# Sliding-window attention and a gated feed-forward: a tail tile loaded and scored later, q and k transfers earlier in SP's queue

## The chip, the cores and the metric

One Trainium2 chip; the program runs on one of its cores. The metric is the device time of one execution in microseconds. Three runs of the kernel before gave 332.56 us as median (332.44 to 333.28). A difference of less than 0.3%, about 1.0 us, can't be told from no change.

The core has a matrix engine (TensorE, "PE"; its weight loads are listed as "PEld"), a vector engine (VectorE, "DVE"), an activation engine (ScalarE, "ACT"), GpSimd ("POOL") and SyncE ("SP"). POOL and SP are used here to issue transfers alone. Each issues in the order of its own queue, and an issue that has to wait holds all that stand behind it.

## The reference

```python
q, k, v: (8, 8, 576, 64)                       # batch, heads, positions, head size
scores = scale * q @ k^T                       # per batch and head
rel  = pos[:, None] - pos[None, :]
mask = (rel >= 0) & (rel < 128)                # causal, a window of 128
scores = where(mask, scores + slope[h] * -|rel|, -1e9)
attn = softmax(scores) @ v
x = attn as (8 * 576, 512)
g = x @ w_gate;  val = x @ w_val               # 512 -> 1536
out = (silu(g) * val) @ w_out                  # 1536 -> 512
```

## The kernel before, in words

**Tiles and units.** A batch has 576 positions: four tiles of 128 and a rest of 64. Batches are taken in pairs, `s` = 0 to 3. A pair has nine tiles of 128 rows: four of the one batch (p = 0 to 3), four of the other (p = 4 to 7), and one, p = 8, that holds the two rests, 64 rows of each: the **tail tile**. So there are 36 tiles; tile 9s + p has that number as its **rank**, and attention goes through them as **units** of the same numbers. Ranks 8, 17, 26 and 35 are tail tiles; 17 is that of batches 2 and 3.

**What a unit scores.** Keys of tile p are needed by the queries of tile p and of tile p + 1. A unit's pass multiplies its keys with two query tiles in one go (line 327, output `ps`), so unit 13 needs k 13, q 13 and q 14. Units with p = 3 and p = 7 end a batch and take one query tile (`scores_128`, line 394, output `psc`). The tail's queries are also scored against the last full tile of each batch (`scores_two`, line 359), and the tail against itself (`scores_128` once more, key `(s, "c")`). In pair 0 both stand at unit 8. In pairs 1 to 3 the tail against itself is scored along with unit p = 3, and `scores_two` along with unit p = 7; unit p = 8 then scores nothing, and its steps are empty lists. The scores go through ACT (exponential) and DVE (mask); `weighted` multiplies them with v, `x_transposed` puts the result into `xT`.

**Feed-forward.** It runs in blocks n = 0 to 8 of 512 rows: block 2s + b is one batch's four tiles, so block 3 takes units 13 to 16, and block 8 takes the four tail tiles. Each block multiplies `xT` with the gate and value weights (line 488), and its output projection (line 636) runs among the next block's products. Blocks 6 to 8 use other products (line 726). Attention and feed-forward are both generators, and `everything` deals out their steps: from step 60 on, attention gets 54 of its steps for 34.5 of the other's. From there PE's order is the order in which the program is written. What a unit yields, empty steps too, counts in this rate.

**How q, k and v come in.** POOL issues the loads (lines 191 and 197), rank by rank, at unit i up to rank i + 7 (`loads_to`); k and q go to staging tiles `kn` and `qn`, five of each. For a tail tile, `load_v` alone is called in its turn, and its k and q are loaded with rank 9s + 3 (`load_qk(rank + 5)`); those of rank 8 are written out by hand. A tail tile takes two transfers of 64 KB for each of k, q and v, another tile one of 128 KB.

From rank 11 on, k and q are transposed by transfers that SP issues (line 253), out of `kn` and `qn` into `kT` (12 places) and `qT` (9). `order` is the list of these transposes: in pair 0 the tail's stand at the end, in the others behind the first four tiles. `ahead(i)`, called at unit i, issues all that `due` puts at i + 4 or less (`AHEAD`); a tail's are due five ranks before their number, together with p = 3. `need[i]` says how many of the list must be out before unit i is scored.

**SP's queue** is written out by hand from unit 7 on: at each unit the transposes of `ahead(i)`, then the transposed result of unit i (line 451; units 8, 9 and from 13 on go this way, 10 to 12 through PE), then finished output rows (line 543).

Of the kernel before, what the change touches and what calls it, by code (L numbers as in the profile page):

```python
# [21 lines left out]
AHEAD = 4  # L22
# [13 lines left out]
SECOND = 5.5  # L36
RATE = 54.0
FIXED_FROM = 60
LATE = 13
VAL_COPIED_FROM = 2  # L40
CLOSE_TO = 13
# [15 lines left out]
def kernel(  # L57
# [65 lines left out]
    msk = consts.tile([P, H, P], FP16, name="m_c")  # L123
# [64 lines left out]
    def load_v(rank):  # L188
        va[rank] = va_all[rank % NV]
        for (p0, p1), src in source(v, rank):  # L190
            nc.gpsimd.dma_start(va[rank][p0:p1, :, 0:D], src)  # L191
# [40 lines left out]
    order = []  # L232
    for s in range(NSUP):
        tails = [("k", 9 * s + 8), ("q", 9 * s + 8)]
        for half in (0, 4):
            order += [(name, 9 * s + half + r) for name, r in zip("kqqkqkqk", (0, 0, 1, 1, 2, 2, 3, 3))]
            order += tails if half == (0 if s else 4) else []
    need = [18 * s + n for s in range(NSUP)
            for n in ((3, 5, 7, 10, 13, 15, 17, 18, 18) if s else (3, 5, 7, 8, 11, 13, 15, 16, 18))]

    def due(rank):

        return rank - 5 if rank % 9 == 8 and rank > 8 else rank

    last_qk = []

# [13 lines left out]
    def begin_scores(i, q4, par, pool=None, tag="a", bufs=4):  # L260

        ps = (pool or ps_a).tile([P, 2, 256], FP32, name="ps", tag=tag, bufs=bufs)
        begun[i, q4, par] = ps
        o = 4 * q4 + 2 * par
        nc.tensor.matmul(ps, idm, bias[:, o:o + 2, :], start=True, stop=False)
# [23 lines left out]
    def scores(i):  # L289

        s, p = units[i]
        def tails():
            return scores_128(s, 8, 8, (s, "c"), msk, unit=i, more=True)

        def together(one, two):
            return [one[0] + two[0]] + one[1:] + two[1:]

        if p == 8:
            return [[]] * 3 + (together(scores_two(s, i), tails()) if s == 0 else [[]] * 2)
        if p in (3, 7):  # L300
            own = scores_128(s, p, p, (s, p), reg[:, :, 0:P], i < FIRST, i)
            return own if s == 0 else together(own, tails() if p == 3 else scores_two(s, i, True))
        ks = (9 * s + p) % NK
        banks = []
        early_tile = i < FIRST
        e = epool.tile([P, H, 256], FP16, name="ex", tag="ex", bufs=4)
        ex[(s, p)] = e

        def products():
            scored[0] = True  # L310
            close.open()
            for q4 in range(2):
                if early_tile:
                    for n in ((q4, 1 - q4) if i < 2 else (q4,)):
                        for par in range(2):
                            if (i, n, par) not in begun:
                                begin_scores(i, n, par)
                    two = [begun[i, q4, par] for par in range(2)]
                else:
                    two = [ps_a.tile([P, 2, 256], FP32, name="ps", tag="a") for _ in range(2)]  # L320
                banks.append(two)
                for j in range(2):
                    pair = 2 * q4 + j
                    for par in range(2):
                        rows = slice(64 * par, 64 * par + 64)
                        with close.behind_first(i):
                            close.put(nc.tensor.matmul(two[par][:, j, :], kT[rows, ks, pair, :],  # L327
                                                       qT[rows, p:p + 2, pair, :],
                                                       start=(j == 0 and not early_tile), stop=(j == 1)))

        def act(q4, par):
            o = 4 * q4 + 2 * par
            nc.scalar.activation(e[:, o:o + 2, :], banks[q4][par], AF.Exp, scale=scale)  # L333

        def mul(q4):
            if early_tile:
                return
            o = slice(4 * q4, 4 * q4 + 4)
            nc.vector.tensor_mul(e[:, o, :], e[:, o, :], reg[:, o, :])  # L339

        return [[products], [lambda: act(0, 0)], [lambda: act(0, 1), lambda: mul(0)],
                [lambda: act(1, 0)], [lambda: act(1, 1), lambda: mul(1)]]

    def scores_two(s, i, more=False):

        ks = [(9 * s + kt) % NK for kt in (3, 7)]
        banks = []

        def products():
            scored[0] = True  # L350
            banks.extend(ps_a.tile([P, 4, P], FP32, name="psc", tag="a") for _ in range(2))
            if not more:
                close.open()
            for j in range(4):
                for n in range(2):
                    for par in range(2):
                        rows, half = slice(64 * par, 64 * par + 64), slice(64 * n, 64 * n + 64)
                        with close.behind_first(i):
                            close.put(nc.tensor.matmul(banks[par][:, j, half], kT[rows, ks[n], j, :],
                                                       qT[rows, 8, j, half], start=(j == 0 and n == 0),  # L360
                                                       stop=(j == 3 and n == 1)))

        def act(par):
            nc.scalar.activation(two_halves[:, 4 * par:4 * par + 4],
                                 banks[par].rearrange("k h (a q) -> k h a q", a=2), AF.Exp, scale=scale)

        def mul():
            nc.vector.tensor_mul(two_halves, two_halves, two_msk.unsqueeze(2).broadcast_to([P, H, 2, 64]))

        return [[products], [lambda: act(0)], [lambda: act(1), mul]]  # L370

    def scores_128(s, kt, qt, key, m, early_tile=False, unit=0, more=False):

        ks = (9 * s + kt) % NK
        banks = []
        e = epool.tile([P, H, P], FP16, name="exc", tag="exc", bufs=4)
        ex[key] = e

        er4 = e.rearrange("k (a par b) q -> k a par b q", a=2, par=2)

        def products():
            scored[0] = True
            banks.extend(ps_a.tile([P, 4, P], FP32, name="psc", tag="a") for _ in range(2))
            if not more:
                close.open()
            for par in range(2 if early_tile else 0):
                nc.tensor.matmul(banks[par].rearrange("k (a b) q -> k a b q", a=2), idm,
                                 bias.rearrange("k (a par b) q -> k a par b q", a=2, par=2)
                                 [:, :, par, :, 0:P], start=True, stop=False)
            for j in range(4):  # L390
                for par in range(2):
                    rows = slice(64 * par, 64 * par + 64)
                    with close.behind_first(unit):
                        close.put(nc.tensor.matmul(banks[par][:, j, :], kT[rows, ks, j, :], qT[rows, qt, j, :],
                                                   start=(j == 0 and not early_tile), stop=(j == 3)))

        def act(par):
            nc.scalar.activation(er4[:, :, par], banks[par].rearrange("k (a b) q -> k a b q", a=2),
                                 AF.Exp, scale=scale)

        return [[products], [lambda: act(0)],
                [lambda: act(1), lambda: early_tile or nc.vector.tensor_mul(e, e, m)]]
# [492 lines left out]
    loaded = done_t = 0  # L895

    def loads_to(r):
        nonlocal loaded
        while loaded <= min(r, NR - 1):
            rank = loaded  # L900
            if rank % 9 == 8:
                load_v(rank)
            else:
                load(rank)
            if rank % 9 == 3:
                load_qk(rank + 5)
            loaded += 1

    by_dma = [n for n in range(len(order)) if order[n][1] >= QK_DMA_FROM]
# [9 lines left out]

    def ahead(i):  # L920

        while by_dma and due(order[by_dma[0]][1]) <= min(i + AHEAD, loaded - 1):
            transpose(by_dma.pop(0))

    def run(steps):
# [46 lines left out]
    def attention():  # L972
# [5 lines left out]
        for i in range(FIRST, last + 1):  # L978
            late = i >= LATE
            if i == QUEUE_FROM:  # L980
# [77 lines left out]
    loaded = 11  # L1058
# [28 lines left out]
    def everything():  # L1087
# [13 lines left out]
        for step in steps:  # L1101
            if step >= FIXED_FROM and fixed is not None:
                fixed.enter_context(tc.manual_schedule(engines=ENGINES["pe"]))
# [50 lines left out]
```

## Time and profile before

| | |
|---|---|
| median of three runs | 332.56 us |
| the profiled execution | 333.68 us |
| its span, first to last instruction | 331.9 us |
| mean granted clock of TensorE | 0.997 |
| PE busy | 321.0 us, 2911 matmuls |
| DVE busy | 261.6 us |
| ACT busy | 221.4 us |
| loads by POOL's queue | 18.62 MB in 118880 packets |
| transfers by SP's and ACT's queues | 19.35 MB in 48048 packets |

The page cuts the span into 40 slices of 8.3 us and gives each engine's busy share in tenths. Its waits name for each engine the line that waited, what it waited for, the sum, the number of waits and the longest. A timeline line gives the start in us, the duration, the engine, the line of the kernel and the operation, output <- input, and in brackets the idle time ahead of it with what ended it; "xN" says that N instructions were merged into one line. SPq is SP's queue: its durations are those of issuing, and a transfer lands later. Landing times of single transfers come from the completion counts in the trace.

### The profile page before, as it was taken

The numbers are of one execution on the slowest core, as the hardware profiler recorded it, in microseconds if no ns is written. First come the engines' busy times: TensorE is split into PE (matmuls) and PEld (weight loads), VectorE is DVE, ScalarE is ACT, GpSimd is POOL, SyncE is SP. The second block draws the span as 40 slices with busy tenths as digits, with TensorE's granted clock in tenths as the row PEclk, the third lists the DMA queues.
The fourth block names the chain that finished last, engine by engine and source line by source line (L and its number), as shares of the span: only waits on it lengthen the run. The fifth ranks groups of instructions, "written<-read, shape, count | busy, mean of one in ns | idle before, by whom it ended". The sixth has DMA issues, their size and how long they took to land. (4 is left out here: it accounts for less than half of the span.)

```text
span 331.9 us, 7661 instructions
## 1 busy us (share of the span) xinstructions
PE 321.0 (97%) x2911; PEld 215.3 (65%) x2911; DVE 261.6 (79%) x638; ACT 221.4 (67%) x438; POOL 111.3 (34%) x138
## 2 busy tenths in 40 slices
PE   8999999999799999999999999999999999999994
PEld 4665465444356665656655655565788888888883
DVE  4678879999597689887998799997854976765783
ACT  4976777365586678777677768753577766777650
POOL 8967777396572535545335100000000000000000
PEclk9999999999999999999999999999999999999998
DMA  9999999999999999999999993113100101001014
GB/s 152 170 181 176 173 178 169 123 121 171 154 150 197 142 163 155 189 136 175 157 144 187 139 182 81 46 28 85 65 32 34 64 2 63 34 35 64 2 63 129
DMA packets 167654, 39.09 MB, mean 118 GB/s; under 512 B 155456, under 2 KB 163264, under 8 KB 167616
## 3 DMA queue, kind: packets, MB, share of 16 engines
q0 software_dynamic: 118880, 18.62, 79.2%
q1 hardware_dynamic: 48048, 19.35, 33.9%
q10 hardware_dynamic: 688, 0.62, 0.6%
q8 instruction: 23, 0.38, 0.5%
q14 instruction: 15, 0.12, 0.1%
HBM read 37.91 MB, written 9.44 MB: 143 GB/s over the span
## 5 line engine op out<-in xcount | busy, mean ns | idle before, releaser
L488 PE MATMUL pv<-xT,wv_sb 128*128 128x512 f16 (+2 forms) x312 | 76.6, 363 | 0.3 <-DVE uu L507 0.2
L488 PE MATMUL pg<-xT,wg_sb 128*128 128x512 f16 (+2 forms) x324 | 76.5, 355 | 0.4 <-DVE hT L515 0.3
L506 ACT ACTIVATE tt<-pg 128x512 f16<-128x512 f32 x68 | 41.7, 614 | 26.5 <-PE pg L488 25.1
L333 ACT ACTIVATE ex<-ps 128x512 f16<-128x512 f32 x96 | 51.0, 612 | 7.6 <-PE ps L327 7.6
L507 DVE SCALAR_TENSOR_TENSOR uu<-tt,pg 128x512 f16<-128x512 f16 x67 | 45.7, 683 | 8.3 <-ACT tt L506 7.9
L197 POOL DMA_DIRECT2D kn<-in_k_dram x39 | 33.3, 854 | 44.0 <-DMA kT<-kn 31.9
L488 PEld LDWEIGHTS <-wg_sb 128*128 128x128 f16 x324 | 29.6, 98 | 26.2 <-issue 2.6
L636 PEld LDWEIGHTS <-hT 128*128 128x128 f16 x384 | 37.0, 98 | 10.0 <-issue 1.0
L488 PEld LDWEIGHTS <-wv_sb 128*128 128x128 f16 x312 | 27.4, 98 | 22.9 <-issue 2.3
L520 ACT CAST hT<-pv 128x512 f16<-128x512 f32 x44 | 26.0, 592 | 19.4 <-PE pv L488 19.3
L197 POOL DMA_DIRECT2D qn<-in_q_dram x39 | 33.3, 860 | 15.4 <-DMA qn<-in_q_dram 8.5
L191 POOL DMA_DIRECT2D va<-in_v_dram x40 | 34.2, 861 | 10.6 <-DMA va<-in_v_dram 4.1
L339 DVE TENSOR_TENSOR ex<-ex,m_reg 128x1024 f16<-128x1024 f16 x42 | 28.9, 689 | 7.7 <-ACT ex L333 7.5
L636 PEld LDWEIGHTS <-S 128*128 128x128 f16 x288 | 27.6, 98 | 7.9 <-issue 1.1
L432 DVE TENSOR_TENSOR x<-av,rec 128x256 f16<-128x256 f32 x72 | 29.0, 421 | 0.6
L636 PE MATMUL po<-T,hT 128*128 128x256 f16 x192 | 26.1, 273 | 0.0
L636 PE MATMUL po<-T,S 128*128 128x256 f16 x192 | 25.9, 273 | 0.0
L521 DVE TENSOR_TENSOR hT<-uu,hT 128x512 f16<-128x512 f16 x44 | 18.5, 421 | 4.0 <-ACT hT L520 3.8
L780 DVE TENSOR_TENSOR hT<-s,v 128x512 f16<-128x512 f16 x18 | 7.6, 424 | 17.7 <-ACT s L779 17.7
L428 PEld LDWEIGHTS <-ex 128*128 128x128 f16 x384 | 17.6, 98 | 5.7 <-issue 1.2
L428 PE MATMUL av<-va,ex 128*128 128x65 f16 x384 | 19.2, 193 | 0.7 <-ACT ex L333 0.3
L327 PE MATMUL ps<-qT,kT 64*128 64x256 f16 x192 | 15.3, 271 | 2.8 <-DMA qT<-qn 2.0
(138 smaller groups left out, 556.4 us busy)
## 6 DMA issues: line engine op xcount, KB each, us to landing
out_dram<-osb SPq DMA_DIRECT2D x32, 256.0 KB, 2.3
va<-in_v_dram POOLq DMA_DIRECT2D x32, 128.0 KB, 10.3
qn<-in_q_dram POOLq DMA_DIRECT2D x31, 128.0 KB, 9.7
kn<-in_k_dram POOLq DMA_DIRECT2D x31, 128.0 KB, 8.6
wg_sb<-in_moe_w_gate_dram POOLq DMA_DIRECT2D x6, 256.0 KB, 7.6
wo_sb<-in_moe_w_out_dram POOLq DMA_DIRECT2D x3, 512.0 KB, 8.2
wv_sb<-in_moe_w_val_dram POOLq DMA_DIRECT2D x5, 256.0 KB, 8.1
kn<-in_k_dram POOLq DMA_DIRECT2D x8, 64.0 KB, 9.3
```

Of the source, the lines that this page charges most:

```text
L191: nc.gpsimd.dma_start(va[rank][p0:p1, :, 0:D], src)
L197: nc.gpsimd.dma_start(t_[p0:p1], src)
L333: nc.scalar.activation(e[:, o:o + 2, :], banks[q4][par], AF.Exp, scale=scale)
L339: nc.vector.tensor_mul(e[:, o, :], e[:, o, :], reg[:, o, :])
L428: nc.tensor.matmul(av[:, j, :], w, val, start=(n == 0), stop=(n == len(todo) - 1))
L432: nc.vector.tensor_mul(x[:, 4 * half:4 * half + 4, :], av[:, :, 0:D], rec.broadcast_to([P, 4, D]))
L488: close.after = nc.tensor.matmul(ps[:, c0:c1], w[:, kb, ms], xT[n][:, kb, c0:c1], start=(kb == 0 and c0 == 0), stop=(kb == NKB - 1 and c1 ...
L506: nc.scalar.activation(tt, pg[:, c0:c1], AF.Tanh, scale=0.5)
L507: nc.vector.scalar_tensor_tensor(out=uu, in0=tt, scalar=one if (n, m) == PIN else 1.0, in1=pg[:, c0:c1], op0=ALU.add, op1=ALU.mult)
L520: nc.scalar.copy(h, pv)
L521: nc.vector.tensor_mul(h, acted[(n, m)][1], h)
L636: nc.tensor.matmul(dst, a[:, m, cols], b[:, m, :], start=(start and m == 0), stop=(m == HM - 1), skip_group_check=True)
```

## The change

The tail tile of pair 1 (rank 17) is treated as follows. Its k and q are loaded in its own turn, behind rank 16, by `load`, and no longer with rank 12. Its transposes stand at the end of pair 1's part of `order`, and are due at 17 instead of 12. `need` for pair 1 is pair 0's list, except that unit 16 needs all eighteen. The tail is scored against itself at unit 17 in a pass of its own (`more=False`, so it opens a group of its own) instead of along with unit 12; `scores_two` stays at unit 16.

For all pairs from 1 on, a unit with p = 8 now yields three steps for its scores instead of five.

From unit 14 on (`EARLIER_FROM`), `ahead` reaches one rank further, i + 5 in place of i + 4.

```diff
+EARLIER_FROM = 14
@@ order, need, due
-            order += tails if half == (0 if s else 4) else []
+            order += tails if half == (0 if s > 1 else 4) else []
     need = [18 * s + n for s in range(NSUP)
-            for n in ((3, 5, 7, 10, 13, 15, 17, 18, 18) if s else (3, 5, 7, 8, 11, 13, 15, 16, 18))]
+            for n in ((3, 5, 7, 10, 13, 15, 17, 18, 18) if s > 1 else (3, 5, 7, 8, 11, 13, 15, 18 if s else 16, 18))]
     def due(rank):
-        return rank - 5 if rank % 9 == 8 and rank > 8 else rank
+        return rank - 5 if rank % 9 == 8 and rank > 17 else rank
@@ scores(i)
         def tails():
-            return scores_128(s, 8, 8, (s, "c"), msk, unit=i, more=True)
+            return scores_128(s, 8, 8, (s, "c"), msk, unit=i, more=s != 1)
         if p == 8:
-            return [[]] * 3 + (together(scores_two(s, i), tails()) if s == 0 else [[]] * 2)
+            return (tails() if s == 1 else [[]] * 3) + (together(scores_two(s, i), tails()) if s == 0 else [])
         if p in (3, 7):
             own = scores_128(s, p, p, (s, p), reg[:, :, 0:P], i < FIRST, i)
-            return own if s == 0 else together(own, tails() if p == 3 else scores_two(s, i, True))
+            if s < (2 if p == 3 else 1):
+                return own
+            return together(own, tails() if p == 3 else scores_two(s, i, True))
@@ loads_to
-            if rank % 9 == 8:
+            if rank % 9 == 8 and rank > 17:
                 load_v(rank)
             else:
                 load(rank)
-            if rank % 9 == 3:
+            if rank % 9 == 3 and rank > 18:
                 load_qk(rank + 5)
@@ ahead
-        while by_dma and due(order[by_dma[0]][1]) <= min(i + AHEAD, loaded - 1):
+        reach = i + AHEAD + (i >= EARLIER_FROM)
+        while by_dma and due(order[by_dma[0]][1]) <= min(reach, loaded - 1):
```

## The prediction

> **What bounds the kernel now.** I read the page first, then the waits of TensorE, then timelines of TensorE, of SP's queue and of POOL around the one long wait, then the times of single transfers.
>
> ```profile
> PE 321.0 (97%) x2911; PEld 215.3 (65%) x2911; DVE 261.6 (79%) x638; ACT 221.4 (67%) x438; POOL 111.3 (34%) x138
> PE   8999999999799999999999999999999999999994
> DMA  9999999999999999999999993113100101001014
> ```
>
> PE is busy 97% of the span, and the change leaves its matmuls as they are. So it can only win idle time of PE: 331.9 - 321.0 = 10.9 us in all. The slices show where it is: the first, the last, and one in between, a "7" at 83 to 91 us. By windows of 8 us, PE's idle time from 56 us to 320 us is 0.08 + 0.29 + 1.69 + 0.03 + 0.44 + 0.43 + 0.27 + 0.04 = 3.3 us. That is the most that this change can bring, and more than half of it is one wait. PE's waits name it:
>
> ```profile
> PE ps L327 <- DMA qT<-qn: 2.0, 2, 1.6
> PE psc L394 <- PE psc L394: 0.3, 1, 0.3
> ```
>
> ```profile
> 79.28 0.40 PE L394 MATMUL psc<-qT,kT 64*128 64x128 f16 x8
> 79.96 0.38 PE L394 MATMUL psc<-qT,kT 64*128 64x128 f16 x4 [0.29 <-PE psc L394]
> ...
> 83.05 0.27 PE L460 MATMUL px<-idm,x 128*128 128x128 f16 x2
> 84.90 0.39 PE L327 MATMUL ps<-qT,kT 64*128 64x256 f16 x4 [1.58 <-DMA qT<-qn]
> ```
>
> At 79.28 PE scores unit 12 (the psc of its own), at 79.96 the tail tile of batches 2 and 3, and at 84.90 it reaches unit 13, which needs q of ranks 13 and 14. The transposed q of rank 14 lands at 84.77, and PE stood 1.58 us. From there to 320 us PE is close to full, so what is saved here is saved at the end, if nothing new waits.
>
> Why q 14 is late is seen in SP's queue and in POOL:
>
> ```profile
> 62.63 6.65 SPq L253 DMA_TRANSPOSE kT<-kn  x2
> 69.45 1.26 SPq L253 DMA_TRANSPOSE qT<-qn  x1
> 70.82 1.29 SPq L451 DMA_TRANSPOSE xT<-x  x1
> 72.21 1.26 SPq L253 DMA_TRANSPOSE kT<-kn  x1
> 73.56 1.32 SPq L253 DMA_TRANSPOSE qT<-qn  x1
> 74.98 1.56 SPq L451 DMA_TRANSPOSE xT<-x  x1
> 76.64 0.56 SPq L543 DMA_DIRECT2D out_dram<-osb  x1
> 77.29 1.33 SPq L253 DMA_TRANSPOSE qT<-qn  x1
> ```
>
> ```profile
> 63.75 1.48 POOL L197 DMA_DIRECT2D kn<-in_k_dram  x2 [6.63 <-DMA kT<-kn]
> 65.22 1.37 POOL L197 DMA_DIRECT2D qn<-in_q_dram  x2
> 66.56 0.92 POOL L197 DMA_DIRECT2D kn<-in_k_dram  x1
> ```
>
> POOL issues the four halves of the tail's k and q (63.75 to 66.56) ahead of rank 13. SP issues k 12, then stands until the tail's k has landed (67.93), issues its k and q (68.08, 69.45), x of unit 8, k 13, q 13, x of unit 9, a store, and at 77.29 q 14. The load of q 14, issued at 70.05, landed at 77.19: at that point the load holds it, not SP.
>
> **The change, part by part.**
>
> The tail's loads leave their place ahead of rank 13 for the one after rank 16. Four issues go: 66.56 - 63.75 = 2.81 us of POOL. The loads of ranks 13 to 16 go out that much sooner, k 13 landing at 67.3 instead of 70.14, q 13 at 70.0 instead of 72.78, q 14 at 74.4 instead of 77.19. Counted by bytes in place of time, q 14 becomes the 640th KB behind 63.75 us, and the 640th landed at 74.14 before: the same.
>
> The tail's two transposes leave SP's queue there as well (2 x 1.3 us and the stand of 4.0 us). SP is then at x of unit 8 at 63.9 (DVE finished it at 63.57), k 13 at 67.3, q 13 at 70.0, x of unit 9 at 71.3 (finished at 70.99), the store at 72.6, and q 14 at 74.4, 2.9 us sooner. With the 7.5 us that q 14 took before (77.29 to 84.77) it lands at 81.9. PE is free for it at 83.32. The wait of 1.58 us goes, with 1.4 us to spare: **-1.58**. The other end of this term is 0: if loads land when they did, q 14 can go out at 77.2, 0.1 us sooner. I take -1.58, for POOL's queue goes out in order and the bytes ahead of q 14 are gone.
>
> The tail's scores move from unit 12 to unit 17 as a pass of their own. At 79.96 the second pass stood 0.29 us for PE's own first pass; that goes (**-0.29**). A pass of its own pays its entry alone: at 95.52 a score group starts 0.10 us later than the matmuls ahead of it would let it (four take 0.86, from 94.56), and inside one group there is no such gap (102.08 to 102.31). **+0.10**. Its two activations (606 ns) and one DVE product (684 ns) are the ones that stood in unit 12; unit 17's weighting reads them some 6 steps of the feed-forward later, and ACT, at 5 to 6.5 us of each 8 us in this stretch, takes 1.2 us more at unit 17 and as much less at unit 12. Nothing.
>
> Units 17, 26 and 35 take 3 steps in place of 5. The attention's steps are dealt out at a fixed rate to the feed-forward's, so 275 become 269 and the attention is over some 4 feed-forward steps sooner. The work is the same. DVE is 7.97 of 8.00 us busy in two windows here (128 to 136, 160 to 168) while PE does not idle; I take 0, with 0.5 either way for a denser mix.
>
> From unit 14, q and k go out one unit sooner. In unit 13 the tail's pair takes a turn that was empty; unit 14 has four. Later waits of this kind before: 0.44 us, at 193.01, for a transpose issued at 183.39 whose load had landed at 179.23. It can go: **-0.44**; the other end is 0. But it also covers something: with PE 1.8 us sooner, units 23 and 24 would stand without it: q for the scores at 144.18 had landed at 143.19, for those at 150.49 at 149.07.
>
> These transfers are slow because they queue, which the answer for this line of SP shows:
>
> ```profile
> DMA to landing us min/median/max: 2.4/8.0/10.1
> ```
>
> The 2.4 us are from the end of the loads, the 8.0 us from among them. The Trainium skill has a rule against this part (DMA: Bandwidth & Descriptors, section "Issuing engines are not separate DMA queues"): what SP, ACT and POOL issue runs on the same 16 DMA engines and interleaves, so a transpose sent sooner takes its share from the loads. By it this part brings 0, and the sum would be -1.8 instead of -2.2.
>
> The sum: -1.58 - 0.29 + 0.10 - 0.44 = **-2.2 us**. The profiled execution took 333.68 us (span 331.9 and 1.8 around it): 331.5. The median of the runs is 332.56, 1.12 below it, so the time to expect is **330.4 us**. Bounds: all of the 3.3 us idle gives 329.3; all terms at their other ends (0, 0, +0.1, 0, +0.5) give 333.2.
>
> **The rivals.**
>
> *The wait moves on* (to units 14 to 16). q 16 landed at 94.36 and PE scored with it at 95.52, 1.16 us to spare. It now stands 1408 KB behind 63.75; that point was reached at 85.41, against 86.92 for its load before, 1.5 us sooner. PE is 1.8 us sooner: 0.9 to spare. q 17, which was there long before, now loads behind rank 16, at about 89, transposed by 96.8, and unit 16 wants it near 100. If ranks 15 to 17 gain nothing, 1.8 - 1.16 = 0.6 is lost, and a unit 16 that stands 1 us more leaves 0.6 of the gain: 332.0. For it: q 15 and q 16 landed only 0.6 and 1.2 us ahead of their scores; against: the byte count.
>
> *It doesn't arrive*: POOL's loads are held by buffers or landings, not by the four issues; POOL stood 6.63 us just ahead of them. Then q 14 is as late as before, 332.3.
>
> *Slower: x of unit 16 comes behind the tail of batches 4 and 5.* Before, q and k of that tail (rank 26) stood ahead of x of unit 17, which is not wanted until the last block. One unit sooner they stand ahead of x of unit 16, and block 3 needs that at once: its first gate matmul ran at 127.03, x of unit 16 was issued at 111.68 and landed at 119.74. Now SP must first issue q 21, k 21, k 26 and q 26; the load of q 26 landed at 112.64, so x 16 goes out near 114.4 and lands at 122.5. PE wants it at 125: 2.5 us to spare. The point from which it decides is q 26 issued after 115.6. In the staging buffers, five deep, k 26 now takes the one of k 17 instead of k 16, whose transpose lands some 2 us later than that one's did. A stand of POOL such as the 6.63 us at kn of rank 17, repeated here, puts q 26 at 119.2, x 16 at 128.6, and PE stands 3.6 us: -2.2 + 3.6 = +1.4, 334.0 us.
>
> **How the numbers follow.** Forecast 0.60, the moved wait 0.12, no arrival 0.10, slower 0.18. The forecast's own range is 329.5 to 331.3. The range that leaves out no more than 2 in 10 reaches over the two middle cases and the upper bound of the terms: 329.3 to 333.3. A measurement of this kernel tells 0.3% (1.0 us) from no change: below 331.56 is faster, above 333.56 slower. Faster takes the forecast and a sliver of the moved wait, 0.62; slower most of the last case, 0.17; the rest 0.21.
>
> **What would show it.** No wait of unit 13's scores for q; kn of rank 13 issued near 63.75; q 14 issued by SP near 74.4; one psc group at unit 12 and one of eight matmuls between units 16 and 18; no wait at unit 31 (193.01 before). Wrong if PE stands at units 14 to 16 for q, or at block 3's first gate for x, or if the loads of ranks 13 and 14 land no sooner.

## The result and the profile after

The changed kernel is faster, by less than forecast. Over 22 runs each on one chip, its median is 332.37 us and that of the kernel before 334.22 us; the ratio is 0.9954, with an interval of 0.9942 to 0.9967. That is 1.1 to 1.9 us, 1.5 in the middle (the two medians differ by 1.85), where 2.2 was forecast. The forecast time of 330.4 us started from the 332.56 us that three runs of the kernel before had shown; on the chips of the later runs its medians were 332.9 to 334.2, so ratios are compared from here on. On another chip the changed kernel stood at 0.9976 (0.9956 to 0.9996).

The profiled execution took 331.93 us with a span of 330.2 (333.68 and 331.9 before). The page of the changed kernel, busy sums and PE's 40 slices:

```profile
PE 321.3 (97%) x2911; PEld 214.8 (65%) x2911; DVE 261.9 (79%) x638; ACT 220.3 (67%) x438; POOL 111.3 (34%) x138
PE   8999999999999999999999999999999999999994
```

The "7" is gone. PE's waits in the changed kernel have no line for `qT<-qn` any more. Those left that come to 0.5 us or more stand at the start of the kernel, as before, save one, which is new (sum, number, longest):

```profile
PE po L639 <- ACT u2s L665: 0.7, 2, 0.5
```

(Lines of the code are 1 to 3 higher than before.) SP's queue, POOL and PE around unit 13, in timelines of the changed kernel:

```profile
62.41 1.26 SPq L254 DMA_TRANSPOSE kT<-kn  x1
63.76 1.22 SPq L454 DMA_TRANSPOSE xT<-x  x1
69.14 1.19 SPq L254 DMA_TRANSPOSE kT<-kn  x1
70.44 1.21 SPq L254 DMA_TRANSPOSE qT<-qn  x1
71.73 1.25 SPq L454 DMA_TRANSPOSE xT<-x  x1
73.08 0.56 SPq L546 DMA_DIRECT2D out_dram<-osb  x1
73.74 1.33 SPq L254 DMA_TRANSPOSE qT<-qn  x1
```

```profile
63.84 0.88 POOL L198 DMA_DIRECT2D kn<-in_k_dram  x1 [6.86 <-DMA kT<-kn]
64.71 0.88 POOL L198 DMA_DIRECT2D qn<-in_q_dram  x1
```

```profile
79.11 0.40 PE L397 MATMUL psc<-qT,kT 64*128 64x128 f16 x8
...
81.45 0.28 PE L463 MATMUL px<-idm,x 128*128 128x128 f16 x2
81.66 0.39 PE L330 MATMUL ps<-qT,kT 64*128 64x256 f16 x4
```

POOL's wait is still there, 6.86 us (6.63 before), and what leaves behind it is now k of rank 13. SP issues q 14 at 73.74 (77.29 before), the completion counts have it landed at 81.49 (84.77), and PE scores unit 13 at 81.66 (84.90) without standing, 0.17 us behind the landing. The tail's own pass is the group of eight behind unit 16:

```profile
104.92 0.40 PE L397 MATMUL psc<-qT,kT 64*128 64x128 f16 x8
```

**Where the time came from and went.** The same gate and value matmuls of both executions can be set side by side. The changed one starts 0.13 us sooner, by its first loads. At the start of block 2 it is 2.6 us ahead (88.42 against 91.04), at the last of these matmuls 1.7 (233.15 against 234.84). Of the 0.9 us between, 0.4 is the tail's pass, which now runs later (0.33, and 0.10 for its entry). Most of the rest are new waits. To count them all, long and short, I take for each matmul the time from the last one's start beyond the median of that execution for the same pair of lines, and add what is over 0.2 us between 91 and 235 us: **1.54 us before** (0.51 for q at unit 31, 0.59 for DVE's `osb`, 0.44 for DVE's `hT`), **1.99 us in the changed kernel** (0.41 and 0.63 for `u2s`, 0.41, 0.22 and 0.32 at three score passes). The three of before went, and five others came. That is 0.45 us more, so the pass and the waits account for nearly all of the 0.9.

### The profile page after: what moved, and what is told of

Its sections match the earlier page's. It is cut to its first block, busy times and chain, and to the rows that moved or that the text cites. A ratio compares the mean times of both kernels' runs of the same rounds, so it can differ in the third digit from the quotient of the medians.

```text
span 330.2 us, 7678 instructions
## 1 busy us (share of the span) xinstructions
PE 321.3 (97%) x2911; PEld 214.8 (65%) x2911; DVE 261.9 (79%) x638; ACT 220.3 (67%) x438; POOL 111.3 (34%) x138
## 4 chain that ended last, share of the span: by engine, by line
PE 73%; DVE 18%; ACT 4%; issue 3%; DMA 1%; ACTq 0%; DVEq 0%
PE po L639 16%; PE pg L491 13%; PE pv L491 12%; PE gX L729 10%; PE gY L729 5%; DVE uu L510 4%; PE av L431 4%; PE p L639 3%; PE ps L330 3%; PE gZ L729 2%; DVE ex L342 2%; DVE hT L526 2%; DVE x L435 2%; PE po L558 2%; ACT tt L509 1%
## 5 line engine op out<-in xcount | busy, mean ns | idle before, releaser
L491 PEld LDWEIGHTS <-wg_sb 128*128 128x128 f16 x324 | 28.9, 98 | 25.1 <-issue 2.2
L526 DVE TENSOR_TENSOR hT<-uu,pv 128x512 f16<-128x512 f16 x24 | 16.2, 680 | 0.7
```

The costliest lines, as they stand in the source:

```text
L491: close.after = nc.tensor.matmul(ps[:, c0:c1], w[:, kb, ms], xT[n][:, kb, c0:c1], start=(kb == 0 and c0 == 0), stop=(kb == NKB - 1 and c1 ...
```

## The experiments

Each kernel behind the first row was timed in five rounds against the kernel before on its own chip: the next four on one chip, the four from "changed, again" on a second, the last four on a third. The last column is the sum just explained, "standing", from its one profiled execution; it leaves out the wait at unit 13, which lies ahead of 91 us.

| kernel | ratio to the kernel before | interval | standing, 91 to 235 us |
|---|---|---|---|
| changed (first chip) | 0.9954 | 0.9942 to 0.9967 | 1.99 |
| tail only | 0.9987 | 0.9970 to 1.0004 | 2.00 |
| earlier turn only | 1.0002 | 0.9986 to 1.0019 | 0.93 |
| tail's loads early | 1.0032 | 1.0009 to 1.0056 | 2.00 |
| five steps at 17, 26, 35 | 0.9990 | 0.9973 to 1.0006 | 3.24 |
| changed, again | 0.9976 | 0.9956 to 0.9996 | 1.99 |
| as many steps as before | 0.9932 | 0.9911 to 0.9952 | 1.22 |
| step counts only | 1.0045 | 1.0025 to 1.0066 | 1.98 |
| all tails | 1.0043 | 1.0022 to 1.0063 | 3.95 |
| as many steps, no earlier turn | 0.9941 | 0.9924 to 0.9959 | 0.87 |
| rate 52 | 0.9999 | 0.9986 to 1.0012 | 3.13 |
| five steps at unit 12 only | 0.9956 | 0.9940 to 0.9973 | 1.75 |
| all tails, as many steps | 0.9946 | 0.9930 to 0.9962 | 0.61 |

### The tail's part alone

```diff
-EARLIER_FROM = 14
+EARLIER_FROM = 99
```

> The tail of batches 2 and 3 is treated as in the changed kernel; q and k go out at unit i up to rank i + 4 throughout, as before. Theory (the earlier turn carries the gain through): unit 13 no longer waits for q (1.58 us before), PE reaches block 2 about 2.5 us sooner than before, as in the changed kernel, but between 100 and 200 us PE then stands for transposed q or k, 0.5 to 1.5 us in sum, for these landed only 1.0 to 1.4 us ahead of their use before. Ratio to the kernel before 0.997 to 0.999. Rival (the earlier turn is worth nothing): no wait for q or k behind unit 13 beyond the 0.44 us of before, ratio as the change's, 0.9954.

This kernel keeps the changed kernel's step counts. Measured 0.9987. The theory's ratio was met and its mechanism was not: unit 13 stands 0.3 us for q, and behind it PE waits for no q or k at all. Its late waits are, one by one, those of the changed kernel (0.41, 0.41, 0.23, 0.32, 0.63). Of the difference between 0.9987 and 0.9954, then, only these 0.3 us are seen as a wait; and the medians, 332.73 and 332.37 us, are 0.4 apart on two chips.

### The earlier turn alone

```diff
+EARLIER_FROM = 14
@@ ahead
-        while by_dma and due(order[by_dma[0]][1]) <= min(i + AHEAD, loaded - 1):
+        reach = i + AHEAD + (i >= EARLIER_FROM)
+        while by_dma and due(order[by_dma[0]][1]) <= min(reach, loaded - 1):
```

> The kernel before with the earlier turn from unit 14 alone. Theory: unit 13 waits as before (1.6 us), unit 31 (0.44 us) does not; ratio 0.998 to 1.000. Rival (the earlier turn is what gives the gain): ratio near 0.9954. Slower rival (x of unit 16 comes behind the tail of batches 4 and 5): x of unit 16 is issued some 4 us later than the 111.68 us of before; block 3's gate waits only if it lands after about 127 us, and I expect it near 123.

Measured 1.0002. Unit 13 waits as before and unit 31 no longer does; nothing is gained that the runs can tell. The slower rival did not come either: x of unit 16 was issued at 117.58 and landed at 124.81, and block 3's first gate ran at 128.12 without a wait.

### The tail's loads early, the rest as changed

```diff
-            if rank % 9 == 8 and rank > 17:
+            if rank % 9 == 8:
                 load_v(rank)
@@
-            if rank % 9 == 3 and rank > 18:
+            if rank % 9 == 3:
                 load_qk(rank + 5)
```

> The changed kernel, but the k and q of the tail of batches 2 and 3 are loaded with rank 12, ahead of rank 13, as before; they are still transposed and scored late. Theory (POOL's order held q 14): the load of q 14 lands near 77.2 us again, its transpose goes out just behind that, and PE stands 1.3 to 1.6 us at unit 13; ratio 0.999 to 1.001. Rival (SP's queue held it): with the two transposes and the 4 us stand gone from SP's queue, q 14 goes out at 74 to 75 us and unit 13 does not wait; ratio near 0.9954.

Measured 1.0032 (1.0009 to 1.0056), slower than before and above the range of the theory. In this kernel SP's queue is free of the tail and POOL's is not. Its SP queue and PE, from timelines:

```profile
73.67 0.53 SPq L546 DMA_DIRECT2D out_dram<-osb  x1
75.46 1.29 SPq L254 DMA_TRANSPOSE qT<-qn  x1
```

```profile
83.58 0.40 PE L330 MATMUL ps<-qT,kT 64*128 64x256 f16 x4 [1.90 <-DMA qT<-qn]
```

SP is done with the store at 74.2 and stands until 75.46: the load of q 14 landed at 75.41. The transpose lands at 83.45, and PE stood 1.90 us. It stood longer than the 1.58 us of before although q 14 landed 1.3 us sooner, for PE, without the tail's pass, reaches unit 13 some 1.6 us sooner. So POOL's order held q 14, as the prediction's step had it; SP's two transposes and its 4 us stand were only in front of a load that was late in any case. The profiled execution was the longest of its twelve, 337.30 us where the median is 333.85: right behind this wait, from 84.1 us, TensorE's granted clock was 0.5 for 6.83 us. The lines above lie ahead of that.

### Five steps at units 17, 26 and 35

```diff
-            return (tails() if s == 1 else [[]] * 3) + (together(scores_two(s, i), tails()) if s == 0 else [])
+            return (tails() if s == 1 else [[]] * 3) + (together(scores_two(s, i), tails()) if s == 0 else [[]] * 2)
```

> The changed kernel, but a unit with p = 8 in pairs 1 to 3 yields five steps again, so attention is spread over the feed-forward as before (275 steps). Theory (the denser mix costs what is missing of the forecast): the two waits of PE for u2s of ACT (0.41 and 0.64 us beyond an ordinary step, at 100 and 211 us in the changed kernel) go or shrink; ratio near 0.9935 to 0.994. Rival (the step count is nothing): ratio 0.9945 to 0.9965, with other waits of the same size in their place.

Measured 0.999, and the standing grew to 3.24 us: neither theory. The number in the expectation is also wrong. Where a unit scores two passes, `together` joins two lists of three steps to one of five, so in pairs 1 to 3 units with p = 3 and p = 7 had five, not three. Counted so, the kernel before yields 289 steps and the changed one 281: six fewer at units 17, 26 and 35, and two fewer at unit 12, whose pass lost the tail's. This kernel yields 287.

### The changed kernel again

> The changed kernel once more, on the same chip as the three that follow. If the parts tried so far (the tail alone 0.9987, the earlier turn alone 1.0002, the tail and the earlier turn with five steps 0.999) and the whole (0.9954) differ by the chip alone, the whole stands here near 0.998. If the parts work together, it stands at 0.994 to 0.9965 again.

Measured 0.9976, between the two expectations; its interval overlaps the first chip's and the parts'. Its median, 332.44 us, is the first chip's 332.37; the kernel before differs more between chips (334.22 and 333.33).

### As many steps as before

```diff
-            return (tails() if s == 1 else [[]] * 3) + (together(scores_two(s, i), tails()) if s == 0 else [])
+            return (tails() if s == 1 else [[]] * 3) + (together(scores_two(s, i), tails()) if s == 0 else [[]] * 2)
@@ p == 3, s == 1
-                return own
+                return own if s == 0 or p == 7 else own + [[]] * 2
```

> The changed kernel, but every unit yields as many steps as before: five at units 17, 26 and 35, and five at unit 12, whose pass had five with the tail's and has three without (289 in all, where the changed kernel has 281). Theory (the pace makes the late waits): behind unit 14 PE's attention stands at the same places among the feed-forward's products as before; the waits for u2s at 100 and 211 us go, those for osb and hT at 215 and 230 us (0.59 and 0.44) come back; against the kernel before, only the 2 us at unit 13 are gone: ratio 0.994 to 0.996. Rival (fewer steps are part of the gain, as the five-step kernel's 0.999 hints): ratio 0.998 to 1.000.

Measured 0.9932, 331.08 us against 332.44 of the changed kernel on the same chip: **the four places of two empty steps were worth 1.4 us.** The standing falls by 0.8 us, of which 0.2 come back at unit 13, so the traces show less than half of that as waits; where the rest is stays open. The ratio is somewhat below the theory's range, whose lower end lies within the interval. The waits came as expected, `u2s` gone and `osb` and `hT` back. PE's waits here (the third is at unit 13, at 81.84):

```profile
PE po L639 <- DVE osb L644: 0.5, 1, 0.5
PE pg L491 <- DVE hT L518: 0.4, 1, 0.4
PE ps L330 <- DMA qT<-qn: 0.4, 1, 0.4
```

How a shift by two steps makes a wait is seen at unit 16. PE of the changed kernel, then ACT of the same stretch, then ACT and PE of the kernel before at the same place:

```profile
98.17 0.40 PE L362 MATMUL psc<-qT,kT 64*128 64x64 f16 x16
98.50 0.83 PE L639 MATMUL po<-T,S 128*128 128x256 f16 x6
99.17 1.03 PE L491 MATMUL pv<-xT,wv_sb 128*128 128x512 f16 x4
100.44 0.81 PE L639 MATMUL po<-T,S 128*128 128x256 f16 x6 [0.24 <-ACT u2s L665]
```

```profile
98.54 1.08 ACT L401 ACTIVATE exc<-psc 128x512 f16<-128x512 f32 x2
99.50 0.62 ACT L367 ACTIVATE two_ex<-psc 128x512 f16<-128x512 f32 x1
99.97 0.41 ACT L665 ACTIVATE u2s<-po 128x256 f32<-128x256 f32 x1
```

```profile
101.32 0.39 ACT L662 ACTIVATE u2s<-po 128x256 f32<-128x256 f32 x1
```

```profile
100.46 0.82 PE L636 MATMUL po<-T,S 128*128 128x256 f16 x6
101.12 1.03 PE L488 MATMUL pv<-xT,wv_sb 128*128 128x512 f16 x4
102.08 0.40 PE L394 MATMUL psc<-qT,kT 64*128 64x128 f16 x8
102.31 0.40 PE L359 MATMUL psc<-qT,kT 64*128 64x64 f16 x16
102.64 0.83 PE L636 MATMUL po<-T,S 128*128 128x256 f16 x6
```

In the changed kernel the scores fall just ahead of the fourth product (S2 by T2, at 98.50) of the output projection's seven. The fifth (S3 by T3) adds into the same place and must wait until ACT has copied that result to `u2s`. It comes only four matmuls later, and ACT has three of the scores' exponentials to do ahead of the copy, which starts at 99.97; PE starts at 100.44, 0.41 us later than the matmuls ahead of it would let it (the line shows 0.24 of it, for it counts from the modelled end of those). Before, the scores fell later behind the fourth product (at 100.46): ACT copied `u2s` from 101.32 on, before it got the scores (102.08), and the fifth ran at 102.64 without a wait.

### The step counts alone, in the kernel before

```diff
-            return [[]] * 3 + (together(scores_two(s, i), tails()) if s == 0 else [[]] * 2)
+            return [[]] * 3 + (together(scores_two(s, i), tails()) if s == 0 else [])
@@ p in (3, 7)
+            if s == 1 and p == 3:
+                return [one + two for one, two in zip(own, tails())]
```

> The kernel before with the changed kernel's step counts alone (three at units 17, 26 and 35; unit 12 scores both passes in three steps). Rival of the above (fewer steps are part of the gain): ratio 0.996 to 0.998 with the wait at unit 13 still there. Theory (the pace moves waits and gains nothing by itself): ratio 0.999 to 1.002, u2s waits as in the changed kernel.

Measured 1.0045: slower, by 1.5 us, outside both ranges on the theory's side. The late waits are the changed kernel's (0.40, 0.41, 0.22, 0.32, 0.63), and the wait at unit 13 is still there. So the step counts lose time with or without the tail's move. Only 0.4 us of the 1.5 is seen as standing (1.98 against 1.54).

### All tails in their turn

```diff
-            order += tails if half == (0 if s > 1 else 4) else []
+            order += tails if half == 4 else []
```

(and the same in `need`, `due`, `scores` and the loads)

> The changed kernel with the tails of all pairs treated as that of batches 2 and 3: loaded in their turn, transposed last, scored at units 26 and 35 in passes of their own. x of units 16 and 25 then no longer stands behind a tail's transposes. Theory: it stood 3.2 us clear of block 3 in the changed kernel, and the tails of pairs 2 and 3 hold no one, so nothing is to be won: ratio within 0.002 of the changed kernel's on this chip, two passes of their own costing 0.1 us each. Rival (a transfer late behind the four transposes costs something that the waits of the one profile don't show): 0.002 to 0.005 below it.

Measured 1.0043, where no more than 0.002 was expected. PE stands 3.95 us in five places, the longest inside a score pass:

```profile
170.16 0.38 PE L330 MATMUL ps<-qT,kT 64*128 64x256 f16 x3 [1.20 <-DVE osb L644]
```

By itself this could have been the harm of two more passes of their own, or of four steps less (units 21 and 30 now have three). The last run below tells.

### As many steps, without the earlier turn

> The changed kernel with as many steps as before (that variant ran at 0.9932) and without the earlier turn from unit 14. Theory (with PE 2 us sooner, q and k that landed 1.0 to 1.4 us ahead of their scores before come too late unless they go out sooner): PE stands for transposed q at units 23, 24 and 31, 1 to 2 us in sum; ratio 0.996 to 0.999. Rival (the earlier turn is worth nothing, its wait at unit 31 aside): ratio 0.993 to 0.995.

Measured 0.9941, 331.05 us, where the same with the earlier turn had 331.08: the rival. The turn is worth nothing that the runs can tell. Behind unit 13 PE waited once for q, 0.3 us, at unit 31. Units 23 and 24 scored at 142.05 and 148.37, 2.1 us sooner than before, and their q had landed at 139.82 and 145.10, 3.4 and 4.0 sooner, though it was not issued a unit earlier.

### The same pace by another way

```diff
-RATE = 54.0
+RATE = 52.0
```

> The changed kernel (281 steps), its attention dealt out at 52 in place of 54 steps for 34.5 of the feed-forward's, so that it ends about where it ended before the change. Theory (what the changed kernel lacks is lost by pace alone): most of the gain of the variant with 289 steps comes back by this other way, ratio 0.993 to 0.9955, with no wait of 0.6 us for u2s at 211 us. Rival (the place of the empty steps matters, not the pace): ratio 0.997 to 0.998 as the changed kernel's on the last chip.

Measured 0.9999, above the ranges of both: the theory of pace falls. Dealt out more slowly, attention ends late again (its last weighting at 224.3 us; 224.4 before, 218.4 in the changed kernel), yet PE stands at other places, 0.83, 0.97 and 1.33 us at score passes and 0.57 for q at unit 13, and the gain is gone. So a sparser mix alone does not bring the time back. That it is rather the product which the scores fall beside fits the waits of all these traces; the new rate moves every pass, so this run by itself does not show it.

### Five steps at unit 12 only

```diff
-                return own
+                return own if s == 0 or p == 7 else own + [[]] * 2
```

> The changed kernel with five steps at unit 12 and three at units 17, 26 and 35 (283 in all). The variant with three at unit 12 and five at the others stood at 0.999, the one with five at all at 0.9932. If unit 12's two steps are what was lost, this stands at 0.993 to 0.995; if the six of the others, at 0.997 to 0.998; if it is the pace behind unit 17, half way.

Measured 0.9956, 331.52 us, between the expectations. By medians (on two chips) unit 12's two steps bring 0.9 of the 1.4 us. The other six alone, at units 17, 26 and 35 above, brought nothing (332.90 us), so the two do not simply add up. On its own chip this kernel's interval overlaps that of the one with all eight (0.9941).

### All tails, as many steps

> The tails of all pairs treated as that of batches 2 and 3, with as many steps as before. With the changed kernel's kind of step counts this stood at 1.0043, PE standing 0.6 to 1.5 us at three score passes and one weighting for DVE and ACT. Theory (pace): with 289 steps it comes near the 0.9932 of the same variant with one tail moved, 0.992 to 0.995. Rival (more tail passes of their own are the harm): 0.997 to 1.003, with the waits of scores for DVE still there.

Measured 0.9946, 331.08 us: the theory's range. The same three moved tails that ran at 1.0043 with fewer steps run as well as one moved tail, with 0.61 us of standing. So the harm was the missing steps', not the two more passes'.

## Why the prediction was right and wrong, point by point

**The wait at unit 13: its size and its cause right, its margin wrong.** The 1.58 us went, and the second pass's stand of 0.29 us at unit 12 too. That POOL's queue and not SP's held q 14 is shown by the run with the loads alone put back. But there were not 1.4 us to spare. k 13 was issued at 63.84 (63.75 worked out) and q 14 at 73.74 (74.4); q 14 landed at 81.49 (81.9). But PE was there at 81.66 and not at 83.32. The prediction left PE where it had been, though it had itself taken the tail's pass and its stand out of the stretch ahead of unit 13; three of the feed-forward's products, which ran there before, came behind unit 13's first scores as well. With 0.17 us to spare the wait just went, and in four of the runs a part of it was left: 0.15 us (changed, again), 0.26 (tail only), 0.37 (as many steps) and 0.57 (rate 52). The way to the landing had two misses that cancelled, which is luck: k 13 landed at 69.12 and not 67.3, and SP stood for it from 64.98 to 69.14, as long as it had stood for the tail's k before; the load of q 14 landed at 71.86 and not 74.4, and SP came to it at 73.74. Why these loads landed so was not tried.

**The step counts: this step failed.** "Units 17, 26 and 35 take 3 steps in place of 5 ... 275 become 269 ... I take 0, with 0.5 either way." The count was wrong, 289 become 281, for unit 12 loses two as well; and the value was wrong, some 1.4 us instead of 0. The count comes from a misreading of `together`. The value comes from the place where I looked: at how full DVE is, and not at which of the feed-forward's products the scores would now stand beside. What the runs showed in place of 0 are new waits of PE at five places, 1.99 us of standing, two of them for ACT's `u2s` (0.41 and 0.63). On the one chip where both ran, the change brings 0.24% without the counts and 0.68% with them (0.9976 and 0.9932), where the sum had been 2.2 of 332.56 us, 0.66%; on another chip the counts without the earlier turn gave 0.59%. So the other terms together were about as large as the sum said, though not each for its reason. On the first chip, where 1.5 of the 2.2 us came, only 0.7 is missing; the counts were not restored there.

**The earlier turn: its term held and its reason did not.** The 0.44 us at unit 31 did go, but it went in the tail's part alone as well; with the counts kept 0.3 us of it was left without the turn; and neither there nor by itself did the turn gain what the runs can tell. "With PE 1.8 us sooner, units 23 and 24 would stand without it" moved PE and left the transfers where they were. They moved along: without the turn, their q landed 3.4 and 4.0 us sooner than before. That x of an earlier unit stands ahead of them in SP's queue, and comes from PE, would make them follow it, but this was not tried by itself. The Trainium skill's rule (DMA: Bandwidth & Descriptors, section "Issuing engines are not separate DMA queues"), that transfers run on the same 16 DMA engines whichever engine issued them, gave 0 for this part, and 331.05 against 331.08 us agrees with that; how the shares fell is not shown by any run here.

**The moved wait: did not come.** In the changed kernel PE waits for q and k at none of units 14 to 17.

**No arrival: excluded** by the load of q 14, which landed at 71.86 in place of 77.19, and by the unit that no longer waits.

**The slower rival: its steps came true, its end did not.** q 26 was issued at 114.20 (115.6 was the point from which it decides), x of unit 16 behind it at 115.49, where 114.4 had been worked out:

```profile
114.20 1.19 SPq L254 DMA_TRANSPOSE qT<-qn  x1
115.49 1.26 SPq L454 DMA_TRANSPOSE xT<-x  x1
```

x landed at 122.57 (122.5 worked out), and block 3's first gate ran at 125.80: 3.2 us to spare, of 7.3 before. The 6.6 us stand of POOL was not repeated ahead of kn of rank 26.

**The pass of its own: +0.10 us**, and the trace shows it: the four matmuls ahead start at 103.96 and take 0.86, and the pass starts at 104.92. No run takes it alone. Three passes of their own ran as one did on the same chip (331.08 against 331.05 us, the latter without the earlier turn).

**The short landings: a wrong place.** The transposes that landed after 2.4 us are not from the end of the loads: they were issued at 61.37 and 62.63, while POOL stood and issued no load. The last transpose of all, at 196.65, took 3.6 us. Between 72 and 185 us, among loads, they took 7.3 to 10.1; so that they are slow beside loads holds.

## What to carry to other kernels

Where an engine works through two interleaved streams, the count of steps that one yields is part of the schedule, empty steps too: an edit that only drops them can move later passes beside other products. Ask of each pass what the next products wait for, and keep the count when something else is to be measured. And when the bottleneck engine is moved in time, let the transfers that hang on its results move with it before calling them late.

## What the runs showed that I had not expected

Putting the tail's k and q loads back ahead of rank 13 gave a longer time than not having the change at all (1.0032): the wait at unit 13 was there, at 1.90 us, and the new waits of the step counts as well.

The wait at unit 13 did not come alone. In two of the kernels that have it, the profiled execution shows TensorE's granted clock at 0.5 shortly behind it: for 6.83 us from 84.1 us behind a wait of 1.90 us (tail's loads early), and for 3.41 us from 86.4 us behind one of 1.56 us (earlier turn only). In the other traces it is below 1 only behind 328 us, if at all. The mean granted clock of a whole execution tells the same. On the three later chips it was 0.995 or less in 21 of the 122 executions of kernels that have this wait at 1.5 us or more (the kernel before: 15 of 86, all of them 333.69 us or longer). It was so in none of the 111 executions of the others, the changed kernel's on the first chip included. So without the wait the clock was steadier; that the wait brings the lower clock was not tried by itself. On the chip of "changed, again", the kernel before has a median of 333.11 us without such executions and 333.33 with them. That may be a part of why the kernel before spread more from chip to chip (medians 332.91 to 334.22 against 332.37 and 332.44 us); for the first chip the record has no clocks of it.

The fastest kernels of the study, 331.05 to 331.08 us, keep the number of steps; with or without the earlier turn, and with one tail moved or all, they can't be told apart.
